# The opening of a layer-norm, scan and gated-MLP kernel: order of the statistics on ScalarE, and the blocks in which gate weights are loaded

## The chip, the core and the metric

The kernel runs on one core of a Trainium2 chip. Its engines are TensorE (PE, with its weight loads shown apart as PEld), VectorE (DVE), ScalarE (ACT), GpSimd (POOL) and SyncE (SP); the queues of SP, ACT and POOL issue transfers, which all run on 16 DMA engines. The metric is device time of one execution in microseconds (us). The kernel before took 181.65 us, the median of three runs (181.58 to 181.92).

## The reference

Everything starts from one layer norm over rows of 448 features, for 2048 tokens:

```python
xn = _layernorm(x, axis=-1)                       # (x - mean) / sqrt(var + 1e-5)
s  = _A_ref(xn, ...)                              # complex diagonal scan over the tokens, then C and the skip
h  = _sigmoid(xn @ w_gate) * (xn @ w_up)          # 448 -> 1792
g  = _silu(h @ w_down)                            # 1792 -> 448
return x + s * g
```

## The kernel before, in words

**Tiles.** The 2048 tokens are 16 tiles of 128 (t = 0 to 15) and four chunks of 512 (c = 0 to 3). A tile is normalized with tokens on partitions into a row buffer (`g_t` for chunk 0, `xn` later). It is then transposed, so that features lie on partitions, into `xnT`, the moving operand of the products. For chunk 0 PE transposes, into PSUM banks that ACT and DVE copy out; for later chunks a DMA transpose does.

**Gate and up products.** The 1792 columns of `w_gate` (tile `wG`) and `w_up` (`wU`) are seven steps m = 0 to 6 of 256 columns, each filling a PSUM pair `gu` (or the pair `acc`). The 448 features lie in four slices; products use 64 rows of the array at a time, in pairs that run side by side, seven pairs for one step. `ph_mm` (L799) issues three pairs and `z_mm` (L789) one; `front` is three pairs and the `z` pair, `back` the last three.

**How the opening is written.** For chunk 0 the products of steps 0 and 1 are issued tile by tile (`units[t][m]`, 128 tokens) and those of step 2 by two tiles (`pairs`), so that PE can begin when one tile is ready. Steps 3 to 6 and all of `wU` follow as whole steps of 512 tokens. Before the first tile PE runs products on a constant (`warm_mm`, L428), and a few more behind the first transposes (`fill`, L1167).

**Statistics of the first four tiles.** DVE computes mean and variance of tiles 0, 1 and 3 (`bn` L434, `aggr` L440), ACT those of tile 2 (`act_mean` L473, `act_var` L477). ACT takes every root (`root` L469, `act_root` L481); DVE the reciprocal (`recip` L465) and the normalization (`norm` L520). Transposes: tile 0 with whole rows (`pe_transpose` L550, copies L553), tiles 1 to 3 with half rows (`row_transpose` L569). Tile 1 is copied by one instruction (`pair_copy` L559), tiles 2 and 3 by two (`row_copy` L576). `columns` (L608) transposes three parameter vectors on PE, and ACT copies them out (L615).

**What sets the order.** Every operation is added to a plan with an estimated cost and its reads and writes. While `pl.seq` is true, as in the opening, DVE and ACT keep the order in which operations are added; PE always does. Later the planner orders DVE, ACT and POOL by due times that it derives from PE's sequence. Loads on SP, ACT and POOL are chained in the order written; `land` is an estimated landing time for the planner alone. Eight completion semaphores go round the loads of SP and ACT, so a load waits until the load eight places before it has landed. `BLK` cuts each weight matrix into column blocks; each block is two loads (`part` 0 and 1, two feature slices each), and a step needs both parts of its block.

Of the kernel before, what the change touches and what calls it, by code (L numbers as in the profile page):

```python
# [14 lines left out]
ACT = mybir.ActivationFunctionType  # L15
# [6 lines left out]
P = 128  # L22
# [225 lines left out]
def kernel(  # L248
# [101 lines left out]
    gu = [pp.tile([P, 2, 512], FP32, name=f"gu{i}") for i in range(3)]  # L350
# [7 lines left out]
    def load(eng, key, nbytes, o, i, cost=0.45, r=(), rate=230e3, land=0.0):  # L358
        e = {"SP": Q, "ACT": A, "POOL": G}[eng]
        add(eng, cost, lambda: e.dma_start(out=o, in_=i), w=[key] if not isinstance(key, list) else key,  # L360
            r=r, dma=nbytes, chain=True, rate=rate).land = land
# [2 lines left out]
        load(q, [("x", t) for t in range(t0, t0 + n)], n * P * D * 2,  # L364
             x_all[:, t0:t0 + n, :], x_src[:, t0:t0 + n, :], r=r, rate=rate, land=land)

    BLK = {"g": [(0, 2), (2, 4), (4, 7)], "u": [(0, 2), (2, 4), (4, 7)]}

    def load_w(eng, k, b, part, r=(), land=0.0):
        m0, m1 = BLK[k][b]  # L370
        c0, c1, r0 = m0 * 2 * P, m1 * 2 * P, (0, 192)[part]
        load(eng, [("w", k, m, part) for m in range(m0, m1)], 4 * P * (c1 - c0), wgt[k][:, 2 * part:2 * part + 2, c0:c1],
             wsrc[k][r0:r0 + 2 * P, c0:c1].rearrange("(s p) f -> p s f", p=P), cost=0.65, r=r, rate=400e3, land=land)
# [17 lines left out]
    def load_p(eng, k, r=()):  # L391
# [5 lines left out]
    load_x(2, 1, "ACT", land=3.8)  # L397
    add("ACT", 0.05, lambda: A.preload_act_table_set("sqrt_and_others"), w=["sqrttab"], lat=1.3, chain=True)
    load_x(3, 1, "ACT", land=4.3)
    load_w("SP", "g", 0, 0, land=5.2)  # L400
    load_w("SP", "g", 0, 1, land=5.6)
    load_p("POOL", 0)
    load_p("POOL", 1)
    add("POOL", 0.15, lambda: G.memset(ident[:], 0.0), w=["ident"], chain=True)
    add("POOL", 0.4, lambda: G.affine_select(out=ident[:], in_=ident[:], compare_op=ALU.not_equal, fill=1.0, base=0,
                                             pattern=[[-1, P]], channel_multiplier=1), r=["ident"], w=["ident"], chain=True)
    load_w("SP", "g", 1, 0, land=6.3)
    load_w("SP", "g", 1, 1, land=7.2)
    load_w("SP", "g", 2, 0, land=8.4)
    load_w("SP", "g", 2, 1, land=9.6)  # L410
    load_x(4, 2, land=10.4)
    load_x(6, 2, land=11.1)
    add("POOL", 0.1, lambda: G.memset(halfc[:], 0.5), w=["consts"])
# [3 lines left out]
    add("POOL", 0.1, lambda: G.memset(pio2[:], PI / 2), w=["pio2"])  # L417
    add("POOL", 0.6, lambda: G.iota(iota[:, 0:NTAB], pattern=[[1, NTAB]], base=0, channel_multiplier=0,
                                    allow_small_or_imprecise_dtypes=True), w=[("wv", 0)])
    for b in range(3):  # L420
        for part in range(2):
            load_w("SP", "u", b, part, land=(12.0, 12.8, 13.6, 14.5, 15.7, 17.0)[2 * b + part])


    def warm_mm(n, w=512):
        def f():
            for _ in range(n):
                T.matmul(gu[2][:, 0, 0:w], lhsT=ones[:, 0:P], rhs=ones[:, 0:w], start=True, stop=True)  # L428
        add("PE", (0.38 if n > 2 else 0.22) * n * w / 512.0, f, w=[("gu", 2)])
# [7 lines left out]
    def aggr(t):  # L437
        b = t % 3
        o = (mvf if t < TPC else mv)[:, t, :]
        add("DVE", 0.1 if t < TPC else 0.16, lambda: V.bn_aggr(out=o, in_=bst[b][:]), r=[("bst", b)], w=[("mv", t)])  # L440
# [22 lines left out]
    def recip(t0, n):  # L463
        ks = lambda k: [(k, t) for t in range(t0, t0 + n)]
        add("DVE", 0.08, lambda: V.reciprocal(out=rsd[:, t0:t0 + n, :], in_=sdb[:, t0:t0 + n, :]), r=ks("sd"), w=ks("rs"))  # L465

    def root(t, n=1):
        ts = range(t, t + n)
        add("ACT", 0.2, lambda: A.activation(sdb[:, t:t + n, :], mvf[:, t:t + n, 1:2], ACT.Sqrt, bias=epsc[:]),  # L469
            r=[("mv", q) for q in ts] + ["sqrttab", "epsc"], w=[("sd", q) for q in ts], lat=0.16)  # L470

    def act_mean(t):
        add("ACT", 0.62, lambda: A.activation(junk[:], x_all[:, t, :], ACT.Identity, scale=-1.0 / D, accum_out=nmf[:, t, :]),  # L473
            r=[("x", t), "sqrttab"], w=[("nf", t), "junk"])

    def act_var(t):
        add("ACT", 0.7, lambda: A.activation(junk[:], x_all[:, t, :], ACT.Square, bias=nmf[:, t, :], accum_out=sqf[:, t, :]),  # L477
            r=[("x", t), ("nf", t)], w=[("mv", t), "junk"])
# [36 lines left out]
    def norm(t, eng="DVE"):  # L515
        b, o, x = xkey(t), pieces(xbuf(t), 256, 256), pieces(x_all[:, t, :], 192, 256)
        if t < TPC:
            s1, op0 = (nmf[:, 2, :], ALU.add) if t == 2 else (mvf[:, t, 0:1], ALU.subtract)
            e, cost = (V, 0.36) if eng == "DVE" else (G, 0.7)
            add(eng, cost, lambda: e.tensor_scalar(out=o, in0=x, scalar1=s1, scalar2=rsd[:, t, :], op0=op0, op1=ALU.mult),  # L520
                r=[("x", t), ("mv", t), ("rs", t)], w=[("xn", b)])
        else:
            r = [("x", t), ("rs", t), ("nm", t)]
            if t < 2 * TPC:
                add("DVE", 0.36, lambda: V.tensor_scalar(out=o, in0=x, scalar1=rsd[:, t, :], scalar2=nmr[:, t, :],
                                                         op0=ALU.mult, op1=ALU.add), r=r, w=[("xn", b)])
            else:
                add("ACT", 0.7, lambda: A.activation(o, x, ACT.Identity, bias=nmr[:, t, :], scale=rsd[:, t, :]), r=r, w=[("xn", b)])
# [26 lines left out]
    def pair_copy(t, a, eng):  # L555
        js = slice(t * P, t * P + P)
        src = gu[a][:].bitcast(BF16)[:, :, 0:4 * H].rearrange("p h (s j) -> p s h j", j=H)
        e, cost = (A.copy, 0.57) if eng == "ACT" else (V.tensor_copy, 0.45)
        add(eng, cost, lambda: e(out=xnT[0][:, :, js].rearrange("p s (h j) -> p s h j", j=H), in_=src),  # L559
            r=[("gu", a, 0), ("gu", a, 1)], w=[("xnT", 0, t, 0), ("xnT", 0, t, 1)])  # L560

    def row_transpose(t, keys, banks):
        o = xbuf(t)
        tp = [flat(bank.bitcast(BF16)[:, 0:4 * H], 4, H) for bank in banks]

        def f():
            for s in range(4):
                for h, (hs, _, _) in enumerate((LO, UP)):
                    T.transpose(tp[h][:, s, :], o[hs, s * P:s * P + P], ident[hs, hs])  # L569
        add("PE", 0.13, f, r=[("xn", xkey(t)), "ident"], w=keys)  # L570
        return tp
# [16 lines left out]
    def gate(keys, key):  # L588
        add("NONE", 0.0, lambda: None, w=list(keys) + (key if isinstance(key, list) else [key]), lat=0.0)
# [13 lines left out]
    def columns(bank, key):  # L603
        vps = flat(bank, 4, 3)

        def f():
            for i in range(4):
                T.matmul(vps[:, i, :], lhsT=vrow[:, i * P:(i + 1) * P], rhs=ident[0:H, 0:3], start=True, stop=True)  # L608
        vks = [("vrow", k) for k in range(3)]
        add("POOL", 0.2, lambda: G.tensor_copy(out=vrow[:, D:512], in_=vrow[:, 384:D]), r=vks, w=["vdup"])  # L610
        add("PE", 0.15, f, r=["ident", "vdup"] + vks, w=[key])
        pv = sbt("pv", [3, 4], FP32)
        dt_b = C("dt", 4, BF16)
        K["pv"] = pv
        return lambda: add("ACT", 0.2, lambda: A.copy(out=pv[:].rearrange("p k i -> p i k"), in_=vps[:]), r=[key], w=["pv0"])  # L615
# [524 lines left out]
        ssm_pair(c, 2)  # L1140


    warm_mm(10)
    pl.seq = True
    slots0 = [next_gu() for _ in range(3)]
    u2 = slots0[2]
# [1 line left out]
    stats(0)  # L1148
    root(0)
    bn(1)  # L1150
    act_mean(2)
    recip(0, 1)
    aggr(1)
    norm(0)
    root(1)
    act_var(2)
    recip(1, 1)
    norm(1)
    uk, ub = [("gu", u2, 0), ("gu", u2, 1)], [gu[u2][:, 0, :], gu[u2][:, 1, :]]
    ak, ab = [("acc", 0), ("acc", 1)], [acc[0][:], acc[1][:]]  # L1160
    units = [[gu_unit(0, "g", m, slots0[m], t, t + 1) for m in range(2)] for t in range(TPC)]
    pairs = [gu_unit(0, "g", 2, u2, t, t + 2) for t in (0, 2)]

    def fill(n):
        def f():
            for _ in range(n):
                T.matmul(gu[slots0[0]][:, 0, 0:P], lhsT=ones[:, 0:P], rhs=ones[:, 0:P], start=True, stop=True)  # L1167
        add("PE", 0.055 * n, f, w=[("gu", slots0[0])])

    def front(us, start=False):  # L1170
        for u in us:
            ph_mm(u, 0, start=start)
            z_mm(u, False)

    def back(us, stop=False):
        for u in us:
            ph_mm(u, 1, stop=stop)

    pe_transpose(0, ak, ab)
    fill(3)  # L1180
    act_root(2)
    row_transpose(1, uk, ub)
    pair_copy(1, u2, "ACT")
    bn(3)
    recip(2, 1)
    norm(2)
    aggr(3)
    front(units[0], True)
    copy_pv = columns(acc[1][:, 400:412], ("acc", 1))
    copy_pv()  # L1190
    add("NONE", 0.0, lambda: None, r=["pv0", ("xn", 0)], w=["pv"], lat=0.0)
    back(units[0])
    front(units[1])
    root(3)
    tp = row_transpose(2, ak, ab)
    for h in range(2):
        row_copy(2, h, ak[h], tp[h])
    recip(3, 1)
    norm(3)
    back(units[1])  # L1200
    gate(uk, ("gu", u2))
    front(pairs[0:1], True)
    front(units[2])
    tp = row_transpose(3, ak, ab)
    for h in range(2):
        row_copy(3, h, ak[h], tp[h])
    silu_table()
    back(units[2])
    back(pairs[0:1])
    turns()  # L1210
    front(units[3])
    front(pairs[1:])
# [117 lines left out]
```

## Time and profile before

| what | value |
|---|---|
| median of the three runs | 181.65 us |
| the profiled execution's own time | 181.81 us |
| its span, first to last instruction | 180.04 us (the page rounds to 180.0) |
| PE busy | 175.7 us, 98% of the span |
| DVE, ACT, POOL busy | 161.3, 106.3, 27.8 us |
| DMA, mean over the span | 12.76 MB, 71 GB/s |

The profiled execution took 1.77 us more than its span; that part lies outside the first and last instruction. A group's `L` number is a line of the kernel, often a helper's. "Idle before" names what ended an engine's idle time. Ends of PE products are modelled, so their starts are the better guide. The page counts a PE that streams at a low rate as busy like any other.

### The profile page before, as it was taken

The numbers are of one execution on the slowest core, as the hardware profiler recorded it, in microseconds if no ns is written. First come the engines' busy times: TensorE is split into PE (matmuls) and PEld (weight loads), VectorE is DVE, ScalarE is ACT, GpSimd is POOL, SyncE is SP. The second block draws the span as 40 slices with busy tenths as digits, with TensorE's granted clock in tenths as the row PEclk, the third lists the DMA queues.
The fourth block names the chain that finished last, engine by engine and source line by source line (L and its number), as shares of the span: only waits on it lengthen the run. The fifth ranks groups of instructions, "written<-read, shape, count | busy, mean of one in ns | idle before, by whom it ended". The sixth has DMA issues, their size and how long they took to land.

```text
span 180.0 us, 4378 instructions
## 1 busy us (share of the span) xinstructions
PE 175.7 (98%) x1798; PEld 89.6 (50%) x1798; DVE 161.3 (90%) x298; ACT 106.3 (59%) x178; POOL 27.8 (15%) x77
## 2 busy tenths in 40 slices
PE   8899999999999999999999999999999999999993
PEld 2774444454544444445554444455555554455452
DVE  4666999999996888999999999999999999999932
ACT  3789993968289998472226643599122699700210
POOL 5374215000028217800000000000000000000000
PEclk9999999999999999999999999999999999999999
DMA  5999937994000230000000430000010000002130
GB/s 146 367 366 241 151 74 213 270 212 110 0 4 0 58 62 0 0 4 0 0 4 0 84 38 0 0 4 25 5 51 0 4 0 0 28 26 100 60 101 26
DMA packets 23943, 12.76 MB, mean 71 GB/s; under 512 B 14833, under 2 KB 23922, under 8 KB 23922
## 3 DMA queue, kind: packets, MB, share of 16 engines
q1 hardware_dynamic: 23568, 12.24, 27.3%
q10 hardware_dynamic: 290, 0.23, 0.6%
q8 instruction: 14, 0.23, 0.5%
q14 instruction: 7, 0.06, 0.1%
q0 software_dynamic: 64, 0.00, 0.0%
HBM read 7.23 MB, written 1.84 MB: 50 GB/s over the span
## 4 chain that ended last, share of the span: by engine, by line
PE 94%; DMA 2%; DVE 1%; ACT 0%; ACTq 0%; issue 0%; DVEq 0%
PE gu L799 42%; PE gu L1041 19%; PE acc L1041 12%; PE acc L799 9%; PE gu L789 7%; PE gu L1024 3%; DMA x_all<-in_A_x_dram 2%; PE acc L789 1%; PE gu L1065 1%; DVE o_t L1126 0%; ACT junk L473 0%; PE acc L1065 0%; DVE o_t L1120 0%; ACTq L360 0%; DVE g_t L520 0%
## 5 line engine op out<-in xcount | busy, mean ns | idle before, releaser
L799 PE MATMUL gu<-xnT,wU 64*128 64x512 bf16 x312 | 45.3, 376 | 0.0
L799 PE MATMUL gu<-xnT,wG 64*128 64x512 bf16 (+2 forms) x324 | 34.2, 321 | 0.0
L1041 PE MATMUL gu<-wd,hF 64*128 64x448 bf16 x336 | 33.8, 349 | 0.0
L1041 PEld LDWEIGHTS <-hF 64*128 64x128 bf16 x392 | 19.9, 94 | 17.4 <-issue 0.2
L1012 ACT ACTIVATE g_t<-gu 128x448 bf16<-128x448 f32 x14 | 7.1, 541 | 35.6 <-PE gu L1041 25.6
L799 PEld LDWEIGHTS <-wG 64*128 64x128 bf16 x420 | 19.0, 94 | 17.4
L799 PEld LDWEIGHTS <-wU 64*128 64x128 bf16 x336 | 16.5, 94 | 19.1 <-PE gu L799 0.3
L954 DVE TENSOR_TENSOR_SCAN wv<-c_r,st,z 128x512 bf16<-128x512 f32 x18 | 22.9, 1275 | 0.0
L862 DVE SCALAR_TENSOR_TENSOR hF<-sig,gu 128x1024 bf16<-128x1024 f32 x15 | 18.3, 1220 | 4.0 <-PE gu L799 3.7
L799 PE MATMUL gu<-xnT,bT 64*128 64x512 bf16 x144 | 19.2, 376 | 0.0
L854 ACT ACTIVATE sig<-gu 128x1024 f32<-128x1024 f32 x14 | 14.3, 1020 | 6.7 <-PE gu L799 6.6
L1041 PE MATMUL acc<-cT,hT 64*128 64x448 bf16 x168 | 17.9, 349 | 0.0
L905 ACT CAST bus<-gu 128x1024 bf16<-128x1024 f32 x12 | 12.1, 1013 | 4.5 <-PE gu L799 4.2
L1041 PEld LDWEIGHTS <-hT 64*128 64x128 bf16 x196 | 10.0, 94 | 8.6
L799 PE MATMUL acc<-xnT,wG 64*128 64x512 bf16 x96 | 14.2, 376 | 0.0
L799 PEld LDWEIGHTS <-bT 64*128 64x128 bf16 x192 | 9.4, 94 | 8.8
L854 ACT ACTIVATE sig<-acc 128x512 f32<-128x512 f32 x14 | 7.8, 593 | 6.0 <-PE acc L799 5.9
L911 ACT CAST bus<-acc 64x256 bf16<-64x256 f32 (+1 forms) x24 | 8.4, 370 | 2.7 <-PE acc L799 2.5
L789 PE MATMUL gu<-xnT,wU 64*128 64x512 bf16 x52 | 9.9, 376 | 0.0
L789 PE MATMUL gu<-xnT,wG 64*128 64x512 bf16 (+2 forms) x54 | 8.8, 321 | 0.0
L434 DVE BATCH_NORM_STATS2 bst<-x_all 128x6 f32<-128x448 bf16 x11 | 6.4, 613 | 2.6 <-DMA x_all<-in_A_x_dram 2.6
L947 DVE TENSOR_TENSOR ta<-bus,cosT 128x1024 bf16<-128x1024 bf16 x12 | 8.2, 681 | 0.1
(166 smaller groups left out, 274.6 us busy)
## 6 DMA issues: line engine op xcount, KB each, us to landing
wd<-in_B_w_down_dram SPq DMA_DIRECT2D x2, 784.0 KB, 6.6
x_all<-in_A_x_dram SPq DMA_DIRECT2D x6, 224.0 KB, 5.2
wG<-in_B_w_gate_dram SPq DMA_DIRECT2D x4, 256.0 KB, 4.3
wU<-in_B_w_up_dram SPq DMA_DIRECT2D x4, 256.0 KB, 6.3
out_dram<-o_t SPq DMA_DIRECT2D x8, 112.0 KB, 1.7
wG<-in_B_w_gate_dram SPq DMA_DIRECT2D x2, 384.0 KB, 5.1
wU<-in_B_w_up_dram SPq DMA_DIRECT2D x2, 384.0 KB, 7.3
out_dram<-ctmp SPq DMA_DIRECT2D x6, 112.0 KB, 1.7
```

The costliest lines, as they stand in the source:

```text
L434: add("DVE", 0.56 if t < TPC else 0.6, lambda: V.bn_stats(out=bst[b][:], in_=x_all[:, t, :]), r=[("x", t)] + ([("xnT", 0, 3, 1)] if 3 < t ...
L789: row_mm(banks[b], b, lambda: T.matmul(out[b], lhsT=w(b, hs, s), rhs=x(b, hs, s), start=start, stop=False), start)
L799: row_mm(banks[b], h, lambda: T.matmul(out[b], lhsT=w(b, hs, ss[q]), rhs=x(b, hs, ss[q]), start=start and q == 0, stop=stop and q == 2), s ...
L854: add("ACT", act(n), lambda s=s, src=src: A.activation(th[:, s, :], src, ACT.Tanh, scale=0.5), r=keys, w=[tk])
L862: add("DVE", dve1(n), lambda s=s, src=src: V.scalar_tensor_tensor(out=ho[:, s, :], in0=th[:, s, :], scalar=1.0, in1=src, op0=ALU.add, op1= ...
L905: add("ACT", act(1024), lambda: A.copy(out=bus[u][:], in_=gu[slots[pt]][:]), r=key(pt), w=[("bus", u)])
L911: add("ACT", 0.36, lambda ns=ns, d=d, q=q, l=l, i=i: A.copy(out=bus[u][d, l, ns], in_=acc[a3[i]][q, 0:256]), r=[("acc", a3[i])] + ([("bus" ...
L947: dve(dve2(1024), lambda: V.tensor_tensor(out=ta[:], in0=b, in1=cosb, op=ALU.mult), [("bus", u)] + tk, [("ta", ia)])
L954: dve(1.194, lambda k=k: V.tensor_tensor_scan(out=wv[:, k, :], data0=rb, data1=z[:, k, :], initial=(st[pt][:, k, :] if c else 0.0), op0=AL ...
L1012: add("ACT", act(448), lambda: A.activation(g_t[g][:], d, ACT.Silu, scale=0.5), r=[key, "silutab"], w=[("gt", g)])
L1024: T.matmul(d, lhsT=hF[c % 2][:, m, h, js], rhs=wd[:, ft, :], start=(ft == 0), stop=(ft == FT - 1))
L1041: row_mm(bk[b][2], h, lambda: T.matmul(bk[b][1], lhsT=lhs(q, hs, js), rhs=rhs(q, hs), start=not turn and q == 0, stop=turn and q == n - 1) ...
```

## The change

Five things change, all in the opening.

1. `wG` is cut into blocks of steps 0, 1, 2 and 3 to 6 (before: 0-1, 2-3, 4-6), so that six loads of 128 KB and two of 512 KB replace four of 256 KB and two of 384 KB. `wU` is cut into steps 0 to 3 and 4 to 6 (before three blocks): four loads for six.
2. On ACT, tile 1's root comes ahead of tile 2's mean, and the copy of tile 0's second half ahead of tile 2's variance. Tile 1's transposed copy moves from ACT to DVE.
3. On DVE, tile 3's `aggr` comes ahead of tile 2's `norm`.
4. PE takes steps 0 and 1 of tiles 0 and 1 one step at a time, with all products of the two tiles ahead of tile 2's transposes; step 2 of tiles 0 and 1 comes before tile 3's transposes.
5. The ten warm-up products of 512 columns become eight of 512 and five of 128; three fill products become two.

The planner, given this, also reorders some DVE and POOL instructions between about 13 and 35 us (two normalizations of chunk 1 and some skip products move later). In the built program tile 3's load on ACT waits for tile 0's, which it did not before, because eight loads are now ahead of it in the round.

```diff
-    BLK = {"g": [(0, 2), (2, 4), (4, 7)], "u": [(0, 2), (2, 4), (4, 7)]}
+    BLK = {"g": [(0, 1), (1, 2), (2, 3), (3, 7)], "u": [(0, 4), (4, 7)]}
...
-    load_w("SP", "g", 0, 0, land=5.2)
-    load_w("SP", "g", 0, 1, land=5.6)
+    load_w("SP", "g", 0, 0, land=4.7)
+    load_w("SP", "g", 0, 1, land=5.3)
...
-    load_w("SP", "g", 1, 0, land=6.3)
-    load_w("SP", "g", 1, 1, land=7.2)
-    load_w("SP", "g", 2, 0, land=8.4)
-    load_w("SP", "g", 2, 1, land=9.6)
+    for b, part, land in ((1, 0, 5.9), (1, 1, 6.4), (2, 0, 6.9), (2, 1, 7.4), (3, 0, 9.0), (3, 1, 10.5)):
+        load_w("SP", "g", b, part, land=land)
...
-    for b in range(3):
+    for b in range(2):
         for part in range(2):
-            load_w("SP", "u", b, part, land=(12.0, 12.8, 13.6, 14.5, 15.7, 17.0)[2 * b + part])
+            load_w("SP", "u", b, part, land=(13.0, 14.5, 15.7, 17.0)[2 * b + part])
...
-    warm_mm(10)
+    warm_mm(8)
+    warm_mm(5, P)
...
     stats(0)
     root(0)
     bn(1)
-    act_mean(2)
     recip(0, 1)
     aggr(1)
     norm(0)
     root(1)
-    act_var(2)
+    act_mean(2)
     recip(1, 1)
     norm(1)
...
     pe_transpose(0, ak, ab)
-    fill(3)
+    fill(2)
+    act_var(2)
     act_root(2)
     row_transpose(1, uk, ub)
-    pair_copy(1, u2, "ACT")
+    pair_copy(1, u2, "DVE")
     bn(3)
     recip(2, 1)
+    aggr(3)
     norm(2)
-    aggr(3)
-    front(units[0], True)
+    front(units[0][0:1], True)
+    back(units[0][0:1])
+    front(units[1][0:1])
+    front(units[0][1:2], True)
+    back(units[1][0:1])
     copy_pv = columns(acc[1][:, 400:412], ("acc", 1))
+    root(3)
     copy_pv()
...
-    back(units[0])
-    front(units[1])
-    root(3)
+    front(units[1][1:2])
+    back(units[0][1:2])
+    back(units[1][1:2])
+    gate(uk, ("gu", u2))
+    recip(3, 1)
+    norm(3)
     tp = row_transpose(2, ak, ab)
...
-    recip(3, 1)
-    norm(3)
-    back(units[1])
-    gate(uk, ("gu", u2))
     front(pairs[0:1], True)
+    back(pairs[0:1])
+    tp = row_transpose(3, ak, ab)
     front(units[2])
-    tp = row_transpose(3, ak, ab)
     for h in range(2):
         row_copy(3, h, ak[h], tp[h])
     silu_table()
     back(units[2])
-    back(pairs[0:1])
```

## The prediction

> **What bounds the kernel now.** I read the page first, its busy times and its slices.
>
> ```profile
> PE 175.7 (98%) x1798; PEld 89.6 (50%) x1798; DVE 161.3 (90%) x298; ACT 106.3 (59%) x178; POOL 27.8 (15%) x77
> PE   8899999999999999999999999999999999999993
> ```
>
> PE is busy in all but the first two slices and the last. The windows view of PE alone, in long stretches behind the opening, shows that this is solid (stretch, its length, PE busy, granted clock, DMA share, GB/s):
>
> ```profile
> 31.00:71.00 40.00, 40.00 (x398) 1.00 0.37 85
> 71.00:110.00 39.00, 39.00 (x392) 1.00 0.09 15
> 110.00:140.00 30.00, 30.00 (x308) 1.00 0.04 13
> 140.00:172.00 32.00, 32.00 (x303) 1.00 0.10 33
> ```
>
> 40.00 us of 40.00 are busy, and so on. By their starts, no product after 7.40 us comes more than 0.06 us late behind the one before. So time can be won or lost only where PE still waits: in the opening. The chain of work that ended last tells what PE waits for there (start, us, what):
>
> ```profile
> 1.67 3.01 DMA x_all<-in_A_x_dram
> 4.68 0.02 issue
> 4.70 0.67 ACT junk L473 x2
> 5.37 0.20 ACT sdb L469
> 5.57 0.02 issue
> 5.59 0.17 DVE rsd L465
> 5.77 0.03 issue
> 5.79 0.42 DVE g_t L520
> 6.22 0.05 issue
> 6.26 0.29 PE gu L569 x8
> ```
>
> Tile 1's root (L469) stands on ACT behind tile 2's mean (L473), which waits for tile 2's rows until 4.68. Tile 1's variance was ready long before: the DVE timeline has `aggr` from 4.19 for 0.18, so at 4.37. The PE timeline gives the rest:
>
> ```profile
> 0.77 4.42 PE L428 MATMUL gu<-const-bfloat16-1.0 128*128 128x512 bf16 x10 [0.77 <-PEq L1314]
> 4.99 0.63 PE L550 MATMUL acc<-ident,g_t 128*128 128x128 bf16 x4
> 5.41 0.38 PE L1167 MATMUL gu<-const-bfloat16-1.0 128*128 128x128 bf16 x3
> 6.26 0.29 PE L569 MATMUL gu<-ident,g_t 64*128 64x64 bf16 x8 [0.47 <-DVE g_t L520]
> 6.46 0.34 PE L799 MATMUL gu<-xnT,wG 64*128 64x128 bf16 x6
> 11.52 0.38 PE L789 MATMUL acc<-xnT,wG 64*128 64x512 bf16 x2
> ```
>
> Gate products begin at 6.46 and are in stride at 6.53, when ACT's copy of tile 0 (6.12, 0.35 us) is done. The tile-wise part ends at 11.52: 4.99 us, of which 0.08 is a wait at 7.40 for tile 1's copy (ACT L559, 6.59 for 0.59).
>
> **Tile 1's root first.** The same steps, with the gaps of the rows above: variance 4.37, root 0.10 later (tile 0's root began 0.10 after its variance) at 4.47, reciprocal 0.31 later at 4.78, `norm` 0.20 later at 4.98 (DVE has ended tile 0's by 4.69), PE 0.47 later at 5.45. That is 0.81 earlier than 6.26. Behind the root, tile 2's mean still starts at 4.70, when its rows land.
>
> **Warm-up and fill.** Ten products of 512 columns, 0.43 us apart, keep PE until 4.99, though tile 0 is normalized at 4.69. Eight end at 4.13, and five of 128 columns (0.107 apart, as L550 shows: four in 0.63, the last 0.31 of it) at 4.67; with the weight load that waits for `g_t`, the transposes start near 4.85. Four of them and two fills, at 0.107, hold PE until 5.49. Tile 1's transposes then start at 5.49, 0.77 earlier.
>
> **Tile 0's copy first.** DVE's half follows `norm` of tile 1 at 5.31. ACT's half can start when the last transpose (5.17 + 0.31) is out, at 5.52, because ACT ends tile 2's mean near 5.38; 0.35 us makes 5.87, and PE is in stride 0.06 later, at 5.93 against 6.53. **This term is -0.60**; the root's 0.77 is cut by the copy, which is late next. Tile 2's variance (0.65, L477) then runs from 5.79 instead of 5.46, its root at 6.45, reciprocal 6.76, `aggr` of tile 3 between, `norm` of tile 2 from 6.96 to 7.37. Tile 3's root and then the parameter copy (L615) wait on ACT for that `aggr` (about 7.04) and end by 7.46. PE wants both for tile 2's transposes at 7.56 or later. Cover: 0.1 us; without it PE waits what is missing.
>
> **Tile 1's copy on DVE.** Transposed by 5.82. No row shows DVE copying 512 PSUM elements: bounds are 0.29 (DVE, 256 elements) and 0.59 (ACT, 512). I take 0.42, as DVE has half the elements in 0.29 with a fixed part. PE, six pairs at 0.056 after 5.93, comes at 6.26 and waits until 6.29: **+0.03** (0 to 0.20), while the old wait of 0.08 goes: **-0.08**. `bn` of tile 3 behind the copy starts at 6.16 instead of 6.32.
>
> **Gate weights.** Steps 0 and 1 were one block of two 256 KB loads, issued at 1.64 and 2.12, which landed 3.5 and 4.2 us later: at 5.11 and 6.31. Step 0's two halves are now first and have the bytes of the first load: about 5.2, wanted at 5.64: hidden. Step 1 needs its second half at 6.51 (6.29 and four pairs). Bounds: 6.31 if bytes alone count; 7.21 if every load lands 0.70 us after the one before whatever its size, as the 256 KB loads did (6.31, 7.02, 7.74). Between them I go by packets. Those of 1,024 bytes took 46 ns in this trace; 512 bytes (the last store) took 27 ns. Four loads are 64 packets on each engine: 1.73 us against 32 at 46 ns, 1.47: 0.26 later, 6.57, used at 6.62. **PE waits 0.11** (0 to 0.75). I keep nearer the low bound because the loads queue back to back (DMA share above 1.0 from 3.7 us). A rule speaks against this cut: the Trainium skill, "DMA: Bandwidth & Descriptors", section "Rules for kernel authors", would coalesce small transfers, as each pays a fixed cost of about 2 us. By that, two loads more in line would cost some 4 us (an estimate from that page) and the gain be gone; landings 0.70 us apart show here that the fixed part overlaps.
>
> **Other transfers, at nothing.** Step 2 lands at 7.5 against 7.8 wanted. Steps 3 to 6 land at about 10.2 (9.83 before, when SP's issue that waits for it goes on, plus 0.38 for six small loads) against 11.0. `wU`'s first block has the bytes that had landed at 15.07 and is wanted at 16.4. Tile 3's rows, whose issue waits until 2.78 instead of 2.12, land by 6.1 at most against `bn` at 6.16. Tiles 4 and 5 land 0.4 later than 10.69; DVE's idle 1.33 us before 15.69 takes that and the reordered normalizations. On SP the transposes of `bT` and everything behind keep their order. Later, DVE itself waits for PE (1.54 us at 56.00, 0.42 at 110.50), so it follows when PE moves.
>
> **Sum.** -0.60 - 0.08 + 0.03 + 0.11 = -0.54 us, and PE's solid run hands it to the end. The profiled execution (span 180.04 and 1.77 around it, 181.81) becomes 181.27; it stands 0.16 above the median of 181.65, so the forecast for a median is 181.1.
>
> **Rivals.** *Late weights of step 1.* The likeliest leak. Landing at 6.9, midway between the bounds, PE waits 0.44: -0.21, 181.4; at 7.21 it is +0.10, 181.75. For it: nothing shows six short loads in a row. Against: packets.
>
> *A clock that rises after the products begin.* Products of 512 columns start 0.43 us apart in the warm-up and 0.215 (a pair) from 11.5 on; fills at 5.41 are the first closer ones. The doubling came at about 5.5, 0.4 us before my 5.93, although the granted clock prints as 1.00 throughout. If it comes at a moment of its own, above 6.53, both kernels lose half of what lies ahead of it, the new one 0.30 more: -0.24, 181.4. The Trainium skill, "TensorE: Matmul & The Clock Gate", Part 1, says so: a free-running window of about 3.4 us; one execution cannot show it.
>
> *Slower: the new warm-up delays that clock.* PE now pauses from 4.67 to 4.85 and runs short products. If the 4.7 us from the first product (0.77) to the doubling (5.5) begin again at 4.85, the clock rises near 9.6; half rate from 5.93 on costs 1.8 us: +1.3, 182.9. It decides against the change from 7.0 on (1.08 us at half rate). Against it: short fills stood right at the doubling before.
>
> *Nothing gained.* Some later engine holds PE where it was: 181.65. Against: DVE's waits for PE.
>
> **How the numbers follow.** Forecast 0.60; late weights 0.18; clock of its own 0.08; delayed clock 0.08; nothing gained 0.06. A measurement tells about 0.2%, 0.36 us, from no change: faster means below 181.29, slower above 182.01. Faster: the forecast and a little of the second, 0.62. Slower: the delayed clock and rest, 0.10. Same: 0.28. The forecast's own range is 180.95 (no wait at all gives -0.68) to 181.3. The range for 8 in 10 goes up to 181.75, the bound of late weights.
>
> **What would show it.** Right: tile 1's root near 4.5, transposes L567 at 5.5, products L797 in stride at 5.9, one wait of 0.1 near 6.5, the first whole step (L787 on `acc`) at 11.0, and the end earlier by the same. Wrong: step 1's second half landing after 6.9; starts of 128-column pairs 0.107 apart beyond 5.9; a PE wait behind 11 us.

## The result, and the profile after

The changed kernel takes 182.61 us (median of 6 runs, 182.59 to 182.77) against 181.71 us of the kernel before (6 runs beside it): a ratio of 1.0048, 95% interval 1.0035 to 1.0061. It is slower by 0.9 us. I had forecast 181.1 us, with a range up to 181.75; the forecast was wrong, in its sign too.

The page of the changed kernel, its busy times and slices, looks like that of before:

```profile
span 180.9 us, 4382 instructions
PE 176.4 (97%) x1800; PEld 97.8 (54%) x1800; DVE 161.8 (89%) x299; ACT 106.0 (59%) x177; POOL 26.9 (15%) x77
PE   8899999999999999999999999999999999999993
```

PE is "busy" for 0.7 us more and its slices have the same digits: ends of products are modelled, so a product that waits in line looks busy. Starts tell more. The PE timeline of the changed kernel (start, length, line, tile, count; line numbers are 2 lower than before):

```profile
4.79 0.41 PE L548 MATMUL acc<-ident,g_t 128*128 128x128 bf16 x4
5.45 0.29 PE L567 MATMUL gu<-ident,g_t 64*128 64x64 bf16 x8
5.64 0.34 PE L797 MATMUL gu<-xnT,wG 64*128 64x128 bf16 x6
5.81 0.24 PE L787 MATMUL gu<-xnT,wG 64*128 64x128 bf16 x2
6.11 0.75 PE L797 MATMUL gu<-xnT,wG 64*128 64x128 bf16 x12
7.13 0.64 PE L797 MATMUL gu<-xnT,wG 64*128 64x128 bf16 x6 [0.22 <-DMA wG<-in_B_w_gate_dram]
7.99 0.26 PE L787 MATMUL gu<-xnT,wG 64*128 64x128 bf16 x2
8.33 0.51 PE L797 MATMUL gu<-xnT,wG 64*128 64x128 bf16 x12
9.12 0.27 PE L787 MATMUL gu<-xnT,wG 64*128 64x256 bf16 x2
9.46 0.50 PE L797 MATMUL gu<-xnT,wG 64*128 64x256 bf16 x6
12.40 0.40 PE L787 MATMUL acc<-xnT,wG 64*128 64x512 bf16 x2
```

The gate products begin at 5.64 instead of 6.46 and are in stride by 5.72 instead of 6.53: 0.81 us won, more than forecast. Then eight places lose it again. Two products of L787 start at 5.81 and take one step of 0.056 us; the next should start near 5.87 and starts at 6.11. The same happens at 6.51 (inside the group of twelve), 8.33 and 9.46, and in small at 10.59 and 10.86. At 7.13 and again at 7.48 PE waits for weights. By starts the lateness is 0.236, 0.229, 0.253 and 0.225 us in the four large places of the first kind (0.94 together), some 0.04 and 0.10 in the two small ones, and 0.381 and 0.259 for weights (0.64 together). The first whole step (L787 on `acc`) starts at 12.40 instead of 11.52. From there to the end both kernels take 168.5 us (180.94 - 12.40 and 180.04 - 11.52), so the 0.88 is the whole difference. The places account for it to within 0.03: -0.81 + 0.94 + 0.14 + 0.64 = 0.91.

The weights came late in a stretch in which the DMA engines moved little. PE and DMA by windows (stretch, length, PE busy, granted clock, DMA share, GB/s), the kernel before:

```profile
4.00:5.00 1.00, 1.00 (x4) 1.00 1.09 370
5.00:6.00 1.00, 0.79 (x8) 1.00 1.07 363
6.00:7.00 1.00, 0.74 (x29) 1.00 1.05 359
7.00:8.00 1.00, 1.00 (x46) 1.00 1.06 367
```

and the changed one:

```profile
4.00:5.00 1.00, 1.00 (x10) 1.00 0.70 164
5.00:6.00 1.00, 0.86 (x22) 1.00 0.86 232
6.00:7.00 1.00, 0.78 (x16) 1.00 1.10 316
7.00:8.00 1.00, 0.80 (x25) 1.00 0.93 290
```

From 4 to 8 us 1459 KB moved before (the sum of the last column, as GB/s over 1 us is KB) and 1002 KB after. Landings: step 1's halves at 7.08 and 7.43, the block of steps 3 to 6 at 10.33 and 12.04 (its bytes were there by 9.83 before), tile 3's rows at 6.88 instead of 5.42.

The first kind of lateness has its source in the code. Products of 64 rows come in two row halves, and `row_mm` counts for each bank which half wrote last:

```python
        if other and other[0] > seen[0]:
            tc.add_manual_dep(T.nop().ins, other[1].ins.name, SYNC, reason="other rows' product in this bank")
```

`back` of a step writes, with the other row half, into the bank that `front` of the step has just written. So it must wait until that product has come out. In the order of before, products of another step and bank stood between the two. Taken step by step, `back` stands right behind its own `front` (at 6.51 it is `front` of tile 1 behind `back` of tile 0, in the same banks). PE's weight loads, which stand ahead of the products, show the four large waits (who waited for whom; us in total, times, longest):

```profile
PEld L797 <- PE gu L787: 0.8, 3, 0.3
PEld L797 <- PE gu L797: 0.2, 1, 0.2
```

The Trainium skill, "TensorEngine Tiling (Array Packing)", Gotcha 1, says that different row tiles cannot access one PSUM bank at the same time and that software must synchronize; it gives no price, the starts above do: 0.22 to 0.25 us each.

### The profile page after: what moved, and what is told of

Same layout as the page of the kernel before. It is cut to its first block, busy times and chain, and to the rows that moved or that the text cites. A ratio compares the mean times of both kernels' runs of the same rounds, so it can differ in the third digit from the quotient of the medians.

```text
span 180.9 us, 4382 instructions
## 1 busy us (share of the span) xinstructions
PE 176.4 (97%) x1800; PEld 97.8 (54%) x1800; DVE 161.8 (89%) x299; ACT 106.0 (59%) x177; POOL 26.9 (15%) x77
## 3 DMA queue, kind: packets, MB, share of 16 engines
HBM read 7.23 MB, written 1.84 MB: 50 GB/s over the span
## 4 chain that ended last, share of the span: by engine, by line
PE 94%; DMA 2%; SPq 1%; DVE 1%; issue 0%; DVEq 0%
PE gu L797 42%; PE gu L1039 19%; PE acc L1039 12%; PE acc L797 9%; PE gu L787 7%; PE gu L1022 3%; DMA wG<-in_B_w_gate_dram 2%; PE acc L787 1%; SPq L360 1%; PE gu L1063 1%; DVE o_t L1124 0%; PE acc L1063 0%; DVE o_t L1118 0%; PE acc L567 0%; PE acc L1061 0%
## 5 line engine op out<-in xcount | busy, mean ns | idle before, releaser
L797 PE MATMUL gu<-xnT,wU 64*128 64x512 bf16 x312 | 46.2, 376 | 0.0
L797 PE MATMUL gu<-xnT,wG 64*128 64x512 bf16 (+2 forms) x324 | 35.6, 321 | 0.6 <-DMA wG<-in_B_w_gate_dram 0.2
L1039 PEld LDWEIGHTS <-hF 64*128 64x128 bf16 x392 | 21.8, 94 | 15.5 <-issue 0.2
L797 PEld LDWEIGHTS <-wG 64*128 64x128 bf16 x420 | 20.7, 94 | 17.4 <-PE gu L787 0.8
L797 PEld LDWEIGHTS <-wU 64*128 64x128 bf16 x336 | 18.5, 94 | 17.1 <-PE gu L797 0.3
L797 PEld LDWEIGHTS <-bT 64*128 64x128 bf16 x192 | 10.7, 94 | 7.5
L787 PE MATMUL gu<-xnT,wU 64*128 64x512 bf16 x52 | 10.3, 376 | 0.0
L787 PE MATMUL gu<-xnT,wG 64*128 64x512 bf16 (+2 forms) x54 | 9.2, 321 | 0.0
```

The costliest lines, as they stand in the source:

```text
L787: row_mm(banks[b], b, lambda: T.matmul(out[b], lhsT=w(b, hs, s), rhs=x(b, hs, s), start=start, stop=False), start)
L797: row_mm(banks[b], h, lambda: T.matmul(out[b], lhsT=w(b, hs, ss[q]), rhs=x(b, hs, ss[q]), start=start and q == 0, stop=stop and q == 2), s ...
L1039: row_mm(bk[b][2], h, lambda: T.matmul(bk[b][1], lhsT=lhs(q, hs, js), rhs=rhs(q, hs), start=not turn and q == 0, stop=turn and q == n - 1) ...
```

## Experiments

The first theory: the order of products and the supply of weights each cost, in series on PE, and what one frees the other takes. Rivals: one of them is the whole loss. Times are compared with runs of the kernel before on the same chip (medians 181.91, 181.88, 181.97 and 181.81 in the four sets).

**Tile 3's rows issued first** (changed kernel). Their issue had slipped behind SyncE's fourth weight load, into the ninth place of a round of eight, and waited for tile 0's rows.

```diff
+    load_x(3, 1, "ACT", land=4.3)
     add("ACT", 0.05, lambda: A.preload_act_table_set("sqrt_and_others"), ...)
-    load_x(3, 1, "ACT", land=4.3)
```

> The changed kernel with one line moved: tile 3's rows are issued ahead of ScalarE's table load, so that this issue is among the first eight and waits for nobody (it waited 0.7 us for tile 0's rows). Theory A (supply: the stretch from 4.2 to 5.6 us in which the DMA engines were only some 0.6 busy comes from this late issue, and the step-1 weights at 7.08 and 7.43 are late by it): step 1's second half lands at 6.0 to 6.6, PE's two waits for it (0.38 and 0.26) go, the four waits for a product of its own remain; first whole step at 11.7 to 11.9, time 181.9 to 182.2. Theory B (the waits for own products are the whole loss and the loads are late by themselves): step 1 lands after 7.0 again, time 182.5 to 182.7.

Measured: 182.61, ratio 1.0037 (1.0023 to 1.0051). Step 1 landed at 5.90 and 6.62 and its two waits are gone, as theory A said; the four own waits stayed (0.235, 0.228, 0.254, 0.226). But the time did not follow. The PE timeline and the windows:

```profile
11.30 0.68 PE L797 MATMUL gu<-xnT,wG 64*128 64x128 bf16 x12
12.50 0.39 PE L787 MATMUL acc<-xnT,wG 64*128 64x512 bf16 x2 [0.53 <-DMA wG<-in_B_w_gate_dram]
...
6.00:7.00 1.00, 0.87 (x27) 1.00 0.76 138
7.00:8.00 1.00, 0.93 (x34) 1.00 0.75 225
```

The DMA engines now run short from 6 to 8 us, and the last block of gate weights lands at 12.45: PE, ready 0.69 us earlier, waits there. From 4 to 8 us only 923 KB moved. The early lateness had hidden a later one. SyncE, free at 4.66, issued that block at 4.97, when step 0's first half had landed (4.96) and given up its place among the eight of the round.

**Halves kept apart** (changed kernel).

```diff
     front(units[0][0:1], True)
-    back(units[0][0:1])
     front(units[1][0:1])
+    back(units[0][0:1])
+    back(units[1][0:1])
     front(units[0][1:2], True)
-    back(units[1][0:1])
...
     front(pairs[0:1], True)
-    back(pairs[0:1])
     front(units[2])
...
     back(units[2])
+    back(pairs[0:1])
```

> The changed kernel with its loads and ScalarE's order, but the halves of a step's products apart: tile 1's first half stands between the two halves of tile 0 (step 0, then step 1), and tile 2's between the two of the pair. PE's four waits for its own product (0.236, 0.229, 0.253, 0.225) should be gone from the trace under both theories. Theory A: the first two stand ahead of the wait for step 1's weights and only move into it, so 0.48 comes off: 182.1 to 182.2, first whole step at 11.9. Theory B: all 0.94 comes off, 181.6 to 181.75, first whole step at 11.5.

Measured: 182.35, ratio 1.0024 (1.0015 to 1.0033), first whole step at 11.95: 0.45 us won on the changed kernel, the size of theory A. That agreement is chance, since not all that the theory assumed came out. My reading of the code was too coarse: the wait is for the bank, and tile 1's first half of the same step writes the same bank as tile 0's. So two of the four waits stayed (0.236 at 6.94, 0.254 at 8.06); only another step in between covers it. PE did not wait for step 1's weights any more (landed at 7.23, used at 7.28), but 0.35 for tile 1's copy at 6.42 and 0.21 for tile 2's copy at 9.17.

**The loads of before** under the changed order.

```diff
-    BLK = {"g": [(0, 1), (1, 2), (2, 3), (3, 7)], "u": [(0, 4), (4, 7)]}
+    BLK = {"g": [(0, 2), (2, 4), (4, 7)], "u": [(0, 2), (2, 4), (4, 7)]}
...
```

> The changed kernel with the weight loads of the kernel before (two steps in one load, three blocks for each matrix); the order of products and of ScalarE stays as changed. Both halves of the first block land at about 6.3, so the gate products start at 6.35 to 6.45. Theory that the order costs as much as it shows: the four waits for own products, 0.2 to 0.25 each, now all count, none for weights; first whole step at 12.1 to 12.3, time 182.2 to 182.5. Rival (the split loads are the whole loss): first whole step at 11.3, time 181.5.

Measured: 182.89, ratio 1.0064 (1.0041 to 1.0087). The loads alone are not the loss: with the old ones and the new order the kernel is slower still. Its profiled run was 184.56, out of line with the other seven (182.65 to 182.99), so the kernel was traced a second time:

> The changed kernel with the loads of the kernel before, looked at a second time because its profiled run was 1.7 us over its other runs (the granted clock was 0.50 from 7.8 to 11 us). Expected of a run at full clock: four waits of 0.22 to 0.25 for own products, the second behind the wait for weights; first whole step at 12.3 to 12.7; span 180.9 to 181.2.

This one took 184.47 and shows the same oddity; see the last section. The waits for own products are in both traces, but no first whole step at full clock could be read.

**ScalarE's order alone** on the kernel before.

```diff
-    act_mean(2)
     recip(0, 1)
...
     root(1)
-    act_var(2)
+    act_mean(2)
...
     fill(3)
+    act_var(2)
     act_root(2)
```

> The kernel before with ScalarE's order alone: tile 1's root ahead of tile 2's mean, tile 0's copy ahead of its variance; loads, products and warm-up as before. Tile 0's copy ends before 6.0, the first block's second half lands at 6.31, so the gate products start at about 6.37 instead of 6.53 and the rest is as rigid as before: 181.5 to 181.6. Rival (tile 2's variance, root and norm, which come later by the copy, are awaited): 181.7 or more, with a PE wait between 8 and 10 us.

Measured: 181.86, ratio 0.9996 (0.9987 to 1.0006): no difference. The gate products started at 6.44, held by the first block's second half (6.39). Then a wait of 0.29 us at 7.53 took the gain. ACT's timeline shows whose:

```profile
5.65 0.37 ACT L553 COPY xnT<-acc 128x256 bf16<-128x256 bf16 x1 [0.36 <-PE acc L550]
5.92 0.67 ACT L477 ACTIVATE junk<-x_all,nmf 128x448 bf16<-128x448 bf16 x1
6.72 0.30 ACT L481 ACTIVATE sdb<-sqf,epsc 128x1 bf16<-128x1 f32 x1
6.92 0.56 ACT L559 COPY xnT<-gu 128x512 bf16<-128x512 bf16 x1
```

Tile 1's copy (L559) stands behind the variance that was moved. With the copy on ScalarE the reorder is worth nothing; that is what its move to DVE is for.

**The order of products of before** (changed kernel).

```diff
-    front(units[0][0:1], True)
-    back(units[0][0:1])
-    front(units[1][0:1])
-    front(units[0][1:2], True)
-    back(units[1][0:1])
+    front(units[0], True)
...
+    back(units[0])
+    front(units[1])
...
+    back(units[1])
```

> The changed kernel with the products in the order of the kernel before (both steps of tile 0, then both second halves, then tile 1), so that no half stands right behind the half whose bank it adds to; loads and ScalarE's order as changed. Theory (order and supply both cost, and stand in series on PE): no wait for own products, but the second unit, step 1 of tile 0, now stands at 6.05 and waits for the weights that land at about 7.1 and 7.4: one wait of 1.3 to 1.4 us; 4.5 us of products remain from 7.45, so the first whole step is at 12.0 to 12.1, held also by the third block at 12.0: time 182.2 to 182.5. Rival (the order alone is the loss): the wait is short, first whole step at 11.0 to 11.3, time 181.2 to 181.5.

Measured: 182.75, ratio 1.0067 (1.0031 to 1.0103); six of the ten runs lie at 182.28 to 182.77, four at 184.2 to 184.3. In the traced run (182.28, the fastest of the ten) no own wait over 0.05 us is left, step 1 landed at 6.89 and 7.19, the two waits for it make 1.07 us (1.3 to 1.4 forecast) and the first whole step is at 11.98. PE's timeline:

```profile
6.02 0.32 PE L787 MATMUL gu<-xnT,wG 64*128 64x128 bf16 x2
6.94 0.58 PE L797 MATMUL gu<-xnT,wG 64*128 64x128 bf16 x6 [0.60 <-DMA wG<-in_B_w_gate_dram]
11.98 0.38 PE L787 MATMUL acc<-xnT,wG 64*128 64x512 bf16 x2
```

**The price of an own wait** in the kernel before.

```diff
-    front(units[0], True)
+    front(units[0][0:1], True)
+    back(units[0][0:1])
+    front(units[0][1:2], True)
+    back(units[0][1:2])
...
-    back(units[0])
```

> The kernel before with one thing changed: in the first unit, tile 0, each step's second half follows its own first half at once (step 0 whole, step 1 whole) where it came one unit later. Loads, ScalarE and warm-up as before. Theory (a half right behind the half whose bank it adds to costs 0.22 to 0.25 us): two new waits of 0.22 to 0.25 us between 6.8 and 7.7 us, first whole step 0.45 to 0.5 us later, at 12.0, time 0.45 to 0.5 us above the kernel before. Rival (the wait is in the trace but something else would have held PE there): no change in time.

Measured: 182.37 against 181.88, ratio 1.0014 (0.9993 to 1.0036): the median moved by the forecast 0.49, the interval does not exclude zero. The trace has the two waits, 0.235 at 7.15 and 0.227 at 7.78, and the first whole step at 12.14, 0.62 later than before. 0.16 of that is a start at 6.69: tile 2's rows landed at 4.91 instead of 4.68 here, tile 1's root stands behind them, and tile 1's transposes came at 6.49 instead of 6.26. So the price is read from the trace; the time alone leaves it open.

**Both cures at once** (changed kernel; tile 3's rows as in the first experiment, up weights as before).

```diff
-    BLK = {"g": [(0, 1), (1, 2), (2, 3), (3, 7)], ...
+    BLK = {"g": [(0, 1), (1, 2), (2, 4), (4, 7)], ...
...
     front(units[0][0:1], True)
-    back(units[0][0:1])
     front(units[1][0:1])
     front(units[0][1:2], True)
-    back(units[1][0:1])
+    front(units[1][1:2])
...
+    back(units[0])
...
+    back(units[1])
```

> Both cures at once on the changed kernel: tile 3's rows issued ahead of the table load; gate weights in blocks of step 0, step 1, steps 2 and 3, steps 4 to 6 and the up weights in three blocks as before; first halves of tiles 0 and 1 in step 0, then in step 1, then the four second halves. Theory (the changed kernel's start at 5.65 is good, what it lost is waits for own products and supply): first gate product at 5.7, the second unit waits 0.2 to 0.25 for tile 1's copy (6.28), step 1's second half lands at 6.5 to 6.8 against 6.63 wanted, no wait for an own product, steps 2 and 3 by 8.2, steps 4 to 6 by 10.5; first whole step at 10.9 to 11.2, time 181.2 to 181.5 where the kernel before has 181.8. Rival (a split first block leaves the DMA engines empty later whatever follows it): a wait of over 0.3 us for steps 2 to 6 between 8 and 12 us, time 181.7 or more.

Measured: 182.89, ratio 1.0046 (1.0021 to 1.0072): the rival. No own wait is left, but step 1's second half landed at 7.10 (wait 0.31) and steps 2 and 3 came so late that PE waited 0.41 at 9.05; 1179 KB moved from 4 to 8 us. First whole step at 12.11. (Its rest took 0.4 us longer than 168.5, with a mean granted clock of 0.998; where is not known.)

**What makes the engines run short: size of transfers or size of packets?** The kernel before, its first four weight loads each cut in two by rows, so that transfers are halved and packets stay at 1,024 bytes; tile 3's rows ahead of the table load.

```diff
+        for s in range(2):
+            keys = [("w", k, m, part) for m in range(m0, m1)] if s else [("w1", k, b, part)]
+            load(eng, keys, 2 * P * (c1 - c0), wgt[k][:, 2 * part + s, c0:c1],
+                 wsrc[k][r0 + s * P:r0 + s * P + P, c0:c1], cost=0.65, rate=400e3, land=land)
```

> The kernel before; each of the first four gate-weight loads is issued as two loads of half the rows (128 KB, 1024-byte packets as before), and tile 3's rows are issued ahead of the table load, so that they leave at 2.1 as before. Nothing else changes. Theory (pace of issue): the engines run short though the packets are as large as before: 1000 to 1250 KB from 4 to 8 us, the first block's last part lands at 6.6 to 7.2 and PE waits for it, first whole step 0.2 to 0.8 later than 11.5, time 182.0 to 182.7. Rival (the size of the packets, 512 bytes, is what starves them): 1350 KB or more from 4 to 8 us, landings within 0.3 of the kernel before, time 181.7 to 182.0.

Measured: 182.62, ratio 1.0038 (1.0023 to 1.0053). With nothing but these two changes, the windows show the same shortage, and PE waits at 9.37:

```profile
4.00:5.00 1.00, 1.00 (x4) 1.00 1.09 331
5.00:6.00 1.00, 0.93 (x8) 1.00 0.95 294
6.00:7.00 1.00, 0.63 (x24) 1.00 0.81 228
7.00:8.00 1.00, 1.00 (x43) 1.00 0.89 216
...
9.37 0.28 PE L807 MATMUL gu<-xnT,wG 64*128 64x256 bf16 x2 [0.58 <-DMA wG<-in_B_w_gate_dram]
```

1069 KB from 4 to 8 us. The size of packets is not needed for it. SyncE stood still from 4.44 to 4.98 here, waiting for a transfer of the round to land; it did so in the kernel before too (4.64 to 5.13), but with twice the bytes in most of the loads under way. The first block itself was complete at 6.53, so the place of the wait was not the one I named.

**Two queues.** Half of step 0's and step 1's loads on ScalarE's queue, the rest as in the kernel with both cures:

```diff
+    load_w("ACT", "g", 0, 1, land=4.9)
     add("ACT", 0.05, lambda: A.preload_act_table_set("sqrt_and_others"), ...)
-    load_x(3, 1, "ACT", land=4.3)
+    load_w("ACT", "g", 1, 1, land=5.6)
+    load_x(3, 1, "ACT", land=5.9)
```

> The kernel of the previous look with all first halves ahead, but the second halves of step 0's and step 1's weights are issued by ScalarE (around its table load), tile 3's rows behind them, so that two queues issue in the time in which one did; SyncE comes to the load of steps 2 and 3 1.0 us earlier. Theory (the DMA engines ran short from 4 to 8 us because one queue issues a transfer every 0.51 us and the split ones carry 128 KB where the kernel before has 256 KB): some 1350 KB or more moved from 4 to 8 us (before 1459, after 1002), step 1 landed by 6.4, steps 2 and 3 by 8.0; no PE wait over 0.25 us but that for tile 1's copy; first whole step at 10.8 to 11.1; time 181.1 to 181.4 where the kernel before has 181.85. Rival (the 512-byte packets or the second queue itself starve the engines): under 1200 KB from 4 to 8 us, step 1 after 6.8, time 181.8 or more.

Measured: 189.04, ratio 1.0401 (1.037 to 1.0432), far outside both. ACT's timeline:

```profile
3.95 0.38 ACTq L360 DMA_DIRECT2D wG<-in_B_w_gate_dram  x1
5.04 0.35 ACTq L360 DMA_DIRECT2D x_all<-in_A_x_dram  x1
5.49 0.30 ACT L468 ACTIVATE sdb<-mvf,epsc 128x1 bf16<-128x1 f32 x1 [1.62 <-DMA wG<-in_B_w_gate_dram]
```

The two issues waited for places in the round (until 3.93, tile 1's rows, and 5.01, step 0's first half), and tile 0's root behind them on ScalarE came at 5.49 instead of 3.79. That is 1.7 of some 7 us. PE then had no product from 4.9 to 6.5, and the full clock came only at 16.14 in this trace (4.86 in the changed kernel), so most of the opening ran at half pace. It says that an issue that can wait must not stand ahead of work on an engine that others wait for; whether two queues feed the engines better it does not say.

**What remains when loads and order are put back.** Changed kernel with loads and order of products of before; ScalarE's order and DVE's copy stay; nine fills ahead of the gate products.

```diff
     row_transpose(1, uk, ub)
+    fill(9)
```

> The changed kernel with the loads and the order of products of the kernel before; ScalarE's order and VectorE's copy of tile 1 stay, and nine short fill products stand ahead of the gate products, so that TensorE is not idle while it waits for the first block. In the look at ScalarE's order alone the gate products started at 6.44, when the first block was there, and tile 1 came 0.29 late, since its copy stood on ScalarE behind tile 2's variance (it began at 6.92). Theory (what the change does on ScalarE and VectorE is right, its loads and its order of products lose the gain): start at 6.4 to 6.5, no wait over 0.1 after it, first whole step at 11.3 to 11.45, span 179.85 to 180.0, time 0.05 to 0.25 below the kernel before. Rival: another wait takes the place of tile 1's copy, time as the kernel before or above.

Measured: 181.99 against 181.81, ratio 1.0012 (0.9997 to 1.0027). The trace has a start at 6.26, earlier than forecast, and then what was forecast: no wait over 0.1, first whole step at 11.33, span 179.86 (0.18 below before), and 1454 KB moved from 4 to 8 us. The time does not show the gain that was forecast. The traced run was the fastest of the twelve (181.63), and its block landed early: in the traces of this study that landing lies between 6.19 and 6.69, and these 0.2 us are inside that.

**Tile 3's rows behind the first block** (the same with six fills).

```diff
-    load_x(3, 1, "ACT", land=4.3)
...
     load_w("SP", "g", 0, 1, land=5.6)
+    load_x(3, 1, "SP", land=6.0)
```

> As the kernel of nine fills, with six, and tile 3's rows (112 KB) issued on SyncE's queue behind the first block of gate weights instead of on ScalarE's ahead of it. Theory (the first block is held by bytes ahead of it): its second half lands 0.2 to 0.35 earlier, at 6.0 to 6.15, tile 3's rows at 6.3 to 6.6; start of the gate products 6.1 to 6.2, first whole step at 11.0 to 11.2, time 0.3 to 0.5 below the kernel before. Rival (landings follow the issue, not the bytes ahead, or tile 3's later rows are awaited): block at 6.3 again or a wait behind 8 us; time as the run beside it.

Measured: 181.87, ratio 0.9993 (0.9972 to 1.0013). The rows landed at 6.42, as asked, but the block at 6.21, no earlier than with the rows ahead of it (6.19): the rival. In this pair of traces, 112 KB ahead of the block were not what held it.

Side by side (us; own waits are those over 0.2; the last column is what remains of the span behind the first whole step):

| kernel | ratio | own waits | KB, 4 to 8 us | first whole step | rest |
|---|---|---|---|---|---|
| before | 1 | 0 | 1459 | 11.52 | 168.5 |
| changed | 1.0048 | 4 | 1002 | 12.40 | 168.5 |
| rows issued first | 1.0037 | 4 | 923 | 12.50 | 168.5 |
| halves apart | 1.0024 | 2 | 1018 | 11.95 | 168.5 |
| order of before | 1.0067 | 0 | 1166 | 11.98 | 168.5 |
| loads and order of before | 1.0012 | 0 | 1454 | 11.33 | 168.5 |

Measured from the last row, the changed order with the old loads (1.0064) adds 0.0052, about 0.95 us, or 0.7 if only the seven close runs count (182.88 / 181.91 = 1.0053); its four own waits are 0.94 in the changed kernel's trace. The changed loads with the old order (1.0067) add 1.0 us, or 0.4 if only the six close runs count (182.5 / 181.88 = 1.0034). Both together (1.0048) add 0.65: less than the sum, since the waits for step 1 are 1.07 us with the old order and 0.64 behind the first two own waits. Each alone makes the kernel slower, and putting only one of them back does not win the gain; the first theory stands.

## Why the prediction was wrong

*Tile 1's root first: right.* Root 4.45, reciprocal 4.78, `norm` 4.98, PE 5.45, against 4.47, 4.78, 4.98 and 5.45.

*Warm-up and fill, tile 0's copy: right, and larger than said by luck.* The four transposes of tile 0 took 0.41 us instead of 0.63, so products already ran at double pace there. ACT's copy started at 5.24, not 5.52, and the term was -0.81 instead of -0.60. But the pace doubles at a moment of its own. Up to tile 1's copy PE has the same products in the changed kernel and in four of the experiments. Yet the traces' records of the granted clock begin, with the full clock, at 4.86 in the changed kernel, at 4.83 with tile 3's rows first, and at 6.18, 6.58 and 6.68 with both cures, the halves apart and the order of before. (Ahead of its first record a view prints 1.00.) In the last three, products of 128 columns still started 0.107 apart at 5.9 to 6.0. The rows with the halves apart, for the 0.41 and 0.34 above:

```profile
4.75 0.61 PE L548 MATMUL acc<-ident,g_t 128*128 128x128 bf16 x4
5.71 0.51 PE L797 MATMUL gu<-xnT,wG 64*128 64x128 bf16 x6
```

The products of L787 behind these start at 6.01, against 5.81 in the changed kernel and 6.62 before: with the late doubling the term is -0.61, as forecast.

*Tile 1's copy on DVE: right.* 0.42 us, as taken from the nearer row; PE's wait for it was hidden by an own wait. Where nothing hid it (halves apart, both cures) it was 0.35 us, above the stated 0.20, behind transposes at the slower pace.

*"Taken step by step": the step that failed most is one that the prediction does not have.* I counted the products of the new order as moved, at no cost, and looked only at what data each needs from other engines. I did not ask what each needs from PE itself. The row to look at was in the trace of before: a product of this form takes 0.22 us to come out and the next starts 0.056 after it, so a product that waits for its predecessor costs about 0.2. Four such waits are 0.94 us, more than the whole gain; this alone turns the sign. (Two smaller ones, 0.14 together, come where tile 3's transposes no longer stand between the halves of tile 2, and step 2's products no longer between tiles 2 and 3.)

*Gate weights: mis-sized, 0.11 forecast, 0.64 measured.* The 0.64 lies inside the stated 0 to 0.75 only because PE was late already: step 1 landed at 7.43, past the bound of 7.21, and with the order of before the two waits were 1.07. I carried over a rate: "the loads queue back to back (DMA share above 1.0 from 3.7 us)". That share belonged to loads of 256 KB. SyncE issues one load every 0.51 us in both kernels (1.64, 2.12, 2.63, 3.15). At 256 KB that is up to 509 GB/s, more than the 360 that moved; at 128 KB it is 254. Two rows of the trace of before, divided, would have warned that the engines can run dry, as they did in the kernel before when its loads were halved with unchanged packets. The rule that I weighed against the cut, the Trainium skill, "DMA: Bandwidth & Descriptors", "Rules for kernel authors", pointed the right way, though not by the size I worked out from it: its 4 us became 0.64 us, and the last block 2.2 us late.

*Other transfers, at nothing: wrong, and hidden.* Steps 3 to 6 were to land at 10.2 and landed at 12.04. Tile 3's rows were to land by 6.1 "at most" and landed at 6.88. Neither shows as a large wait in the changed kernel, only because PE was late already; with step 1 on time, the last block cost 0.69 us at 12.50. Costing these at nothing was right for the path as it came out and wrong as a forecast of it.

*The rivals.* "Late weights of step 1" had the right mechanism, at 0.18 and with at most +0.10 us: as priced it could not turn the sign by itself. The clock "that rises after the products begin" had the right mechanism: its moment is not set by the kernel's products, and in the traced run of the changed kernel it fell early, in its favour. A doubling delayed to 9.6 by the new warm-up did not happen; only with two queues, behind a longer pause, was it later (16.14). "Nothing gained" did not happen: the start was gained, and lost again. Of the marks named ahead, step 1 landing after 6.9 was the one that showed; "a wait behind 11 us" came only with tile 3's rows issued first.

*What stays open.* Three things can starve the engines here, and the runs do not fully separate them: the pace of issue, the wait for a place among eight transfers (0.5 us with halved loads, 0.3 with rows first), and nine single packets that took 0.26 to 0.50 us from 4.4 to 5.5 in the changed kernel, where 512 bytes took 27 ns otherwise and 896 bytes 41. The packets in the traces tell something. The first one of step 0 moved 1.65 us after its issue in the changed kernel. With halved loads, 765 of the 768 KB of gate weights that had been issued at least 1.75 us before 6.5 had moved by then: little was left to move, which fits the first two causes. In the changed kernel 332 of 640 KB had moved by 5.5: there bytes were waiting, so its first weak stretch is not for want of issued loads, and its cause stays open. It left when tile 3's rows were issued earlier, and another came at 6 to 8 us. No version here beats the kernel before by more than its interval.

## What to carry to other kernels

When instructions of one engine are put in a new order, ask of each what it needs from that engine's own last result, not only from the others: two dependent products that become neighbours cost the latency that their neighbours used to cover. Before cutting a transfer to get its first part sooner, divide bytes per transfer by the pace of issue in the trace, and count how many may be under way; if the result is below the rate that the engines move, later transfers may pay. And when one wait is removed, read the next landing against its use: here each cure uncovered the one behind it. A gain read from one trace of an opening can be luck: look at the starts of the same products in a second trace, where they differed here by 0.2 us.

## What the runs showed that I had not expected

In both traced runs of the changed kernel with the loads of before the granted clock fell to half for about 3.4 us (7.64 to 11.05, and 7.23 to 10.65), 3.4 us after it had begun at full (4.22 and 3.82), by windows of the second (some of its rows):

```profile
4.00:5.00 1.00, 0.66 (x10) 1.00 1.03 335
6.00:7.00 1.00, 0.27 (x5) 1.00 0.96 314
8.00:9.00 1.00, 1.00 (x28) 0.50 1.07 387
9.00:10.00 1.00, 0.93 (x21) 0.50 1.05 357
11.00:12.00 1.00, 0.93 (x32) 1.00 1.08 374
```

These runs took 184.56 and 184.47, 1.5 to 1.9 us above the seven others of the kernel, about half of the 3.4. In the second, PE had waited 0.50, 0.31 and 1.02 us between 4 and 7 us. The Trainium skill, "TensorE: Matmul & The Clock Gate", Part 1, states a half-rate clock behind an idle window of about 3.4 us, free-running; the length agrees, but PE was never idle for a whole one (0.27 of its time from 6 to 7, 0.66 and 0.75 in the two windows ahead). Four of the ten runs of the order of before with the new loads, in which PE waits 0.9 us at a time, lie at 184.2 to 184.3 as well. They were not traced, but their mean granted clock was 0.989 to 0.990, where the other six have 0.998 or more and the two traced runs 0.988 and 0.991. One run with both cures (184.40) and one of the kernel before (183.79) show 0.988 too. A wait in the opening may thus cost more than its length, by chance of when it falls; that the waits bring the fall about is not shown.
